# Cached attention for one token: the output weights loaded in two large pieces behind the last K

## The chip, the cores and the metric

The kernel runs on one core of a Trainium2 chip. The metric is the device time of one execution in microseconds (us), the median of several runs. The profile is of one such execution; it names the engines PE (TensorE, matmuls; PEld is its weight load), DVE (VectorE), ACT (ScalarE), POOL (GpSimd) and SP (SyncE, which here only issues transfers).

## The reference

Two independent attention blocks, A and B, each with its own input, caches and weights, are computed and their results put side by side. For each of them, with batch B = 8, one query token, D = 1024, H = 32 heads, Sk = 4096 cached positions and Dh = 128, all bf16:

```python
q = (x @ wq).reshape(B, 1, H, Dh).transpose(0, 2, 1, 3)
p = softmax(einsum("bhqd,bhkd->bhqk", q, k_cache) * Dh ** -0.5)
o = einsum("bhqk,bhkd->bhqd", p, v_cache)
y = o.transpose(0, 2, 1, 3).reshape(B, 1, H * Dh) @ wo
```

The output is `concatenate([yA, yB], axis=-1)`, 8 x 1 x 2048. The caches are 4 x 268 MB, the four weight matrices 8.4 MB each; every byte is read once.

## The kernel before, in words

**Slots.** The work is cut into NS = 64 slots, 32 for A and then 32 for B. A slot is one batch entry with a group of eight heads (HP = 8); four groups (NG) of eight batch entries make a block, and the batch entry runs fastest. A slot's K is 8 heads x 4096 positions x 128, 8 MB (8,388,608 bytes), laid out as 128 partitions x 64 KB: sixteen partitions a head, each with T = 256 positions. Its V has the same form. K goes into one of two buffers (`kbuf`, slot number modulo 2), V into the one buffer `vbuf`. "MB" of a load below means 1,048,576 bytes, "KB" 1024.

**One slot.** VectorE multiplies K by the query, spread over all partitions, in four chunks in place (`multiply`, line 352). TensorE sums the products over Dh with sixteen matmuls a chunk against the identity (`add_up`, line 362) into the banks `red`, and VectorE reduces the rest (line 374). After a softmax whose exponentials are eight ACTIVATEs on ScalarE (`exps`, line 390), the probabilities stand ready for P.V (`pv`, line 413), which a slot later multiplies them with V into the bank `oacc`; `copy_o` (line 432) brings it to SBUF, `gather` (line 442) adds the sixteen partitions of a head, `rowsum` (line 396) sums the exponentials, and `heads` (line 455) divides and files the result, on GpSimd, into `ona` (line 457), a buffer for two groups.

**Order.** The program is written out by hand in one list an engine, and waits are worked out from what each operation reads and writes. In the body of slot n (lines 540 to 601) the loads come first: K of slot n, at times a piece of output weights, V of slot n - 1. SyncE issues them in this order and stops at each until its buffer is free. Then the four chunks pass through VectorE and TensorE, P.V of slot n - 1 follows on TensorE, and the exponentials on ScalarE.

**Output weights before.** Each two heads (256 rows of `wo`, 512 KB) are one load into `wob` (`load_wo`, line 322), two rows of 2 KB that are adjacent in memory for each partition, so 4 KB runs. There are 32 such pairs of heads; 28 of them, all but those of the last group of B, are loaded in this way, one in every second slot from slot 10 on and one in slot 63. In such a slot GpSimd picks the two heads (`pick_heads`, line 461), TensorE permutes them to fit the rows (`permute`, line 468, four matmuls), VectorE copies the result (line 474), TensorE multiplies them with the weights (`project`, line 480, eight matmuls through `strips`, which puts the four quarters of the 1024 columns on four strips of partitions), VectorE copies that (line 491) and GpSimd adds it up in `osum` (lines 494 and 497). When A is complete its four output pieces are stored by SyncE (`store`, in slot 44).

**The last slots before.** In slot 63 the last V is issued directly behind V of slot 62, in four parts (half, quarter, two eighths) into the K buffer of slot 62 (`load_v`, lines 306 to 313). P.V of slot 62 frees `vbuf`, and the last group's weights follow there, four loads of 512 KB in 2 KB runs (`load_wo_last`, line 324). Matmuls on the identity whose result nobody reads (`idle`, line 516) fill TensorE's waits. The last projection (`project_last`) goes part by part as these weights land; VectorE adds `osum` (line 507) and SyncE and ScalarE store the second half.

**Loops.** All slots but the first and the last are hardware loops over two slots: slots 1 to 8, and 9 to 62, which differ by the output weights.

Of the kernel before, what the change touches and what calls it, by code (L numbers as in the profile page):

```python
# [143 lines left out]
def _build(nc, caches, out):  # L144
# [15 lines left out]
    CW = D // 4  # L160
    assert Sq == 1 and Dh == 128 and Sk == 4096 and D == 1024 and H % HP == 0 and B == 8 and NP * 2 == B
    assert R * H * Dh == T * Dh and NC == 2
# [3 lines left out]
    with es:  # L166
# [10 lines left out]
        wob = sb("wob", [128, 2, D], BF16)  # L177
# [8 lines left out]
        ona = sb("ona", [128, 2, HP, B], BF16)  # L186
# [7 lines left out]
        ong = sb("ong", [128, 2, B], BF16)  # L194
        onp = sb("onp", [128, 2, B], BF16)
# [7 lines left out]
        xs = wob[:].rearrange("p a n -> p (a n)").rearrange("p (c n) -> p c n", c=NC)  # L203
        xT = orow[:, 0:NC * R * B].rearrange("p (c r b) -> p c r b", c=NC, r=R)
        qrow = [(asb[:].bitcast(BF16), "asb"), (osum[:].bitcast(BF16), "osum")]
        otail = kbuf[:, 1, 0:2 * TB * Dh].bitcast(FP32)
# [30 lines left out]
        for base, mul in ((0, 1), (SEG - 1, -1)):  # L237
            P.add("pool", lambda e, base=base, mul=mul: e.affine_select(
                out=neg[:], in_=neg[:], compare_op=ALU.is_ge, fill=-1e30, base=base,
                pattern=[[-mul * SEG, HP]], channel_multiplier=mul), reads=["neg"], writes=["neg"])  # L240
        P.add("dve", lambda e: e.memset(ones[:], 1.0), writes=["ones"])
# [11 lines left out]
        def make_xT(c):  # L253
            def emit(e):
                last = None
                for r in range(R):
                    last = e.matmul(sps[:, 256 + r * B:256 + (r + 1) * B], xs[0:B, c, r::R], ident[0:B, 0:B], start=True, stop=True)
                return last
            P.add("pe", emit, reads=[f"xs{c}", "wo", "ident"], banks=["sps"])
            P.add("dve", lambda e: e.tensor_copy(xT[:, c].rearrange("p r b -> p (r b)"), sps[:, 256:256 + R * B]),  # L260
                  writes=["orow"], banks=["sps"])
# [38 lines left out]
        def load_v(m):  # L300
            c, g, b = where(m)
            if m < NS - 1:
                dma("sp", vbuf[:], source(c, 2, b, g), ["v"], "v")
                vplace[m] = (vbuf[:], [("v", 0, T)])
                return
            i, at, parts = NS % 2, 0, []
            for j, w in enumerate((T // 2, T // 4, T // 8, T // 8)):
                name = f"vpart{j}"
                dma("sp", kbuf[:, i, at * Dh:(at + w) * Dh], source(c, 2, b, g)[:, at * Dh:(at + w) * Dh],
                    [name] if j else [name, f"k{i}"], name)  # L310
                parts.append((name, at, w))
                at += w
            vplace[m] = (kbuf[:, i, :], parts)

        def wo_rows(p):
            gi, k = divmod(p, NP)
            c, g = divmod(gi, NG)
            at = (g * HP + 2 * k) * Dh
            return caches[c][4][at:at + 2 * Dh, :]

        def load_wo(p):
            dma("sp", wob[:], wo_rows(p).rearrange("(p j) n -> p j n", j=2), ["wo"], "wo")

        def load_wo_last():
            for k in range(NP):
                name = f"wlast{k}"
                dma("sp", wlast[:, 2 * k:2 * k + 2, :], wo_rows((NC * NG - 1) * NP + k).rearrange("(h p) n -> p h n", p=Dh),
                    [name] if k else [name, "v"], name)
# [99 lines left out]
        def copy_o(m):  # L428
            if m == NS - 2:
                P.add("dve", lambda e: e.tensor_copy(otail, oacc[:]), writes=["k1", "otail"], banks=["oacc"])  # L430
                return
            P.add("act", lambda e: e.activation(osb[:], oacc[:], ACTF.Copy), writes=scores, banks=["oacc"])  # L432

        def gather(m, after=False):
            o = 32 + (m % 2) * HP
            parts = len(vplace[m][1])
            tb, of = (2, olate) if after else (TB, otail if m == NS - 2 else osb)
# [7 lines left out]
            P.add("pe", emit, reads=(["asb"] if after else ["otail"] if m == NS - 2 else scores) + ["sel"], banks=["sps"])  # L445

        def heads(m):
            i = m % 2
            o = 32 + i * HP
            gi, b = divmod(m, B)  # L450
            if m == NS - 1:
                P.add("dve", lambda e: e.tensor_tensor(ona[:, gi % 2, :, b], sps[:, o:o + HP], rl[:, i, :], ALU.mult),
                      reads=[f"rl{i}"], writes=[f"ona{gi % 2}"], banks=["sps"])
# [3 lines left out]
            P.add("pool", lambda e: e.tensor_copy(ona[:, gi % 2, :, b], on[:, i, :]), reads=[f"on{i}"], writes=[f"ona{gi % 2}"])  # L457

        def pick_heads(p):
            gi, k = divmod(p, NP)  # L460
            P.add("pool", lambda e: e.tensor_copy(ong[:], ona[:, gi % 2, 2 * k:2 * k + 2, :]), reads=[f"ona{gi % 2}"], writes=["ong"])

        def permute():
            def emit(e):
                last = None
                for hh in range(2):
                    for j in range(2):
                        last = e.matmul(sps[64 * hh:64 * hh + 64, 64 + j * B:64 + (j + 1) * B], ident[:, j::2], ong[:, hh, :],  # L468
                                        start=True, stop=True, tile_position=(0, 64 * hh))
                return last  # L470
            P.add("pe", emit, reads=["ong", "ident"], banks=["sps"])

        def permuted():
            P.add("dve", lambda e: e.tensor_copy(onp[:].rearrange("p j b -> p (j b)"), sps[:, 64:64 + 2 * B]),
                  writes=["onp"], banks=["sps"])
# [8 lines left out]
        def project():  # L484
            def emit(e):
                strips(e, onp[:, 0, :], wob[:, 0, :], True, False)
                return strips(e, onp[:, 1, :], wob[:, 1, :], False, True)
            P.add("pe", emit, reads=["onp", "wo"], banks=["acc"])

        def projected(p):  # L490
            P.add("dve", lambda e: e.tensor_copy(asb[0:104, :], acc[0:104, 0:CW]), writes=["asb"], banks=["acc"])  # L491
            k = p % (NP * NG)
            if k == 0:
                P.add("pool", lambda e: e.tensor_copy(osum[0:104, :], asb[0:104, :]), reads=["asb"], writes=["osum"])
                return
            dst, name = (orow, "orow") if k == NP * NG - 1 else (osum, "osum")
            P.add("pool", lambda e: e.tensor_tensor(dst[0:104, :], asb[0:104, :], osum[0:104, :], ALU.add),  # L497
                  reads=["asb", "osum"], writes=[name])

        def project_last():  # L500
            g = (NC * NG - 1) % 2
            for k in range(NP):
                def emit(e, k=k):
                    strips(e, ona[:, g, 2 * k, :], wlast[:, 2 * k, :], k == 0, False)
                    return strips(e, ona[:, g, 2 * k + 1, :], wlast[:, 2 * k + 1, :], False, k == NP - 1)
                P.add("pe", emit, reads=[f"ona{g}", f"wlast{k}"], banks=["acc"])
            P.add("dve", lambda e: e.tensor_tensor(orow[0:104, :], acc[0:104, 0:CW], osum[0:104, :], ALU.add),
                  reads=["osum"], writes=["orow"], banks=["acc"])
# [17 lines left out]
        L0, L1, L2 = 1, B + 1, NS - 1  # L526
# [13 lines left out]
        for n in range(NS):  # L540
            m = n - 1
            p = (n - B - 2) // 2 if n >= B + 2 and n % 2 == 0 else NP * (NC * NG - 1) - 1 if n == NS - 1 else None
            if n in (L1, L2):
                for e, at in marks().items():
                    P.loops[e].append((start[e], at, (n - was) // 2))
            if n in (L0, L1):
                start, was = marks(), n
# [30 lines left out]
            add_up(n, 3)  # L578
            reduce(n, 3)
# [20 lines left out]
            if n == B * NG + B + 4:  # L600
                store(0)
# [112 lines left out]
```

## Time and profile before

| What | us |
|---|---|
| median of three runs | 2566.83 (2566.71 to 2567.71) |
| the profiled execution's own time | 2566.92 |
| its span in the profile | 2565.0 |
| busy: PE, DVE, ACT, POOL | 1472.9, 1371.9, 647.2, 314.9 |
| from issue to landing of a 512 KB piece of output weights, median | 51.3 (A), 51.0 (B) |
| from issue to landing of a part of the last group's weights, median | 15.1 |

The span goes from the first to the last instruction; the execution's own time is 1.9 us more. The mean granted TensorE clock was 0.799. In rows of the timeline the columns are start, duration, engine, line, operation, output tile <- input tiles, size and count; a bracket at the end gives the engine's idle time before the row and what ended it. In rows of windows the columns are the stretch and its length, busy time of PE, PEld, DVE, ACT and POOL with the number of instructions, the granted clock, the busy share of the sixteen DMA engines, and GB/s.

### The profile page before, as it was taken

How to read it: one execution, taken by the hardware profiler on the slowest of the kernel's cores; microseconds unless marked ns; L12 is line 12 of the kernel's file. 1: busy time of each engine (PE TensorE's matmuls, PEld its weight loads, DVE VectorE, ACT ScalarE, POOL GpSimd, SP SyncE). 2: the span in 40 equal slices, each digit the busy share in tenths (PEclk: the TensorE clock that was granted, in tenths of full speed). 3: DMA queues.
4: the chain of work that ended last, by engine and by line, in shares of the span. 5: the costliest groups of instructions: out<-in, count | busy, mean ns of one | idle time of the engine just before them, and what ended most of it. 6: DMA issues, size and time to landing. Idle time of an engine off the chain costs nothing.

```text
span 2565.0 us, 19446 instructions
## 1 busy us (share of the span) xinstructions
PE 1472.9 (57%) x9528; PEld 290.1 (11%) x5688; DVE 1371.9 (53%) x969; ACT 647.2 (25%) x1121; POOL 314.9 (12%) x166
## 2 busy tenths in 40 slices
PE   3565565565565555655655556556556565565566
PEld 0101101101111111111110111110101111111102
DVE  3456455465464564554645645546446455465463
ACT  0322322313313223223132132231321322313313
POOL 0101011011011010110110111101101111011010
PEclk8787787787887877878878778778787787787888
DMA  9999999999999999999999999999999999999999
GB/s 425 430 436 432 434 434 432 434 432 433 433 433 431 432 433 433 433 433 433 433 433 433 433 432 434 433 432 432 433 429 439 433 433 432 432 430 432 433 433 392
DMA packets 24445, 1107.54 MB, mean 432 GB/s; under 512 B 2720, under 2 KB 2784, under 8 KB 7408
## 3 DMA queue, kind: packets, MB, share of 16 engines
q1 hardware_dynamic: 24368, 1107.33, 99.9%
q8 instruction: 7, 0.11, 0.0%
q10 hardware_dynamic: 64, 0.04, 0.0%
q14 instruction: 6, 0.05, 0.0%
HBM read 1107.33 MB, written 0.03 MB: 432 GB/s over the span
## 4 chain that ended last, share of the span: by engine, by line
DMA 40%; PE 22%; DVE 18%; another core or an unknown queue 9%; issue 9%; ACT 1%; SPq 0%; DVEq 0%; ACTq 0%
DMA kbuf<-in_A_k_cache_dram 21%; DMA kbuf<-in_B_k_cache_dram 19%; PE red L362 16%; DVE kbuf L352 14%; PE oacc L413 5%; DVE osb L374 2%; ACT prob L390 1%; PE red L516 0%; SPq L223 0%; DVE on L455 0%; DVEq L647 0%; DVE rmax L379 0%; ACT qbc L344 0%; DVE rl L402 0%
## 5 line engine op out<-in xcount | busy, mean ns | idle before, releaser
L352 DVE TENSOR_TENSOR kbuf<-kbuf,qbc 128x8192 bf16<-128x8192 bf16 x256 | 1128.2, 4408 | 807.4 <-DMA kbuf<-in_A_k_cache_dram 363.4
L362 PE MATMUL red<-kbuf,ident 128*128 128x512 bf16 x4096 | 1057.8, 419 | 409.8 <-DVE kbuf L352 206.9
L390 ACT ACTIVATE prob<-osb,bias 128x256 bf16<-128x256 f32 x512 | 598.7, 1583 | 929.3 <-PE oacc L413 894.7
L457 POOL COPY ona<-on 128x8 bf16<-128x8 bf16 x64 | 278.7, 4354 | 1853.6 <-DVE on L455 1853.6
L442 PE MATMUL sps<-sel,osb 128*128 128x8 f32 x504 | 115.6, 358 | 648.4 <-ACT osb L432 648.3
L374 DVE TENSOR_REDUCE osb<-red 128x64 f32<-128x512 f32 x256 | 176.0, 687 | 304.1 <-PE red L362 304.1
L390 ACT ACTIVATION_READ_ACCUMULATOR prob<-osb,bias 128x1 f32 x512 | 252.9, 494 | 0.0
L344 ACT ACTIVATE qbc<-bps 128x256 bf16<-128x256 f32 x32 | 12.3, 384 | 938.9 <-PE bps L340 938.9
L413 PE MATMUL oacc<-vbuf,prob 128*32 128x512 bf16 x4032 | 229.1, 380 | 0.0
L442 PEld LDWEIGHTS sps<-sel,osb 128*128 128x128 f32 x504 | 111.5, 326 | 667.8 <-issue 667.8
L413 PEld LDWEIGHTS oacc<-vbuf,prob 128*32 128x32 bf16 x4032 | 101.8, 97 | 315.2 <-issue 219.0
L362 PEld LDWEIGHTS red<-kbuf,ident 128*128 128x128 bf16 x256 | 25.1, 98 | 974.4 <-issue 948.3
L497 POOL TENSOR_TENSOR osum<-asb,osum 104x256 f32<-104x256 f32 x25 | 18.1, 723 | 309.1 <-DVE asb L491 309.1
L432 ACT ACTIVATE osb<-oacc 128x512 f32<-128x512 f32 x63 | 37.6, 597 | 10.8 <-PE oacc L413 3.8
L396 PE MATMUL sps<-rsum,ones 128*128 128x8 f32 x128 | 36.6, 359 | 5.5 <-ACT prob L390 5.5
L396 PEld LDWEIGHTS sps<-rsum,ones 128*128 128x128 f32 x128 | 34.7, 330 | 6.1 <-ACT prob L390 5.5
L379 DVE TENSOR_REDUCE rmax<-osb 128x1 f32<-128x256 f32 x64 | 26.9, 420 | 7.6
L468 PEld LDWEIGHTS sps<-ong,ident 128*64 128x64 bf16 x112 | 4.1, 109 | 154.9 <-issue 154.9
L380 DVE STREAM_TRANSPOSE tmax<-rmax 128x32 f32<-128x32 f32 x64 | 13.5, 212 | 7.7
L402 DVE RECIPROCAL rl<-sps 128x8 f32<-128x8 f32 x64 | 12.7, 198 | 8.0 <-PE sps L396 8.0
L333 POOL COPY qg<-qT 128x256 bf16<-128x256 bf16 x32 | 12.7, 396 | 28.0 <-DVE qT L286 27.5
L381 DVE TENSOR_REDUCE nmax<-tmax 128x2 f32<-128x32 f32 x64 | 11.9, 186 | 7.6
(59 smaller groups left out, 138.4 us busy)
## 6 DMA issues: line engine op xcount, KB each, us to landing
wob<-in_A_wo_dram SPq DMA_DIRECT2D x16, 512.0 KB, 51.3
wob<-in_B_wo_dram SPq DMA_DIRECT2D x12, 512.0 KB, 51.0
kbuf<-in_B_v_cache_dram SPq DMA_DIRECT2D x1, 4096.0 KB, 42.4
kbuf<-in_B_v_cache_dram SPq DMA_DIRECT2D x1, 2048.0 KB, 47.0
kbuf<-in_B_v_cache_dram SPq DMA_DIRECT2D x2, 1024.0 KB, 49.8
vbuf<-in_B_wo_dram SPq DMA_DIRECT2D x4, 512.0 KB, 15.1
kbuf<-in_A_k_cache_dram SPq DMA_DIRECT2D x32, 50.1
vbuf<-in_A_v_cache_dram SPq DMA_DIRECT2D x32, 31.1
```

What stands on the lines that cost most here:

```text
L352: P.add("dve", lambda e: e.tensor_tensor(kv, kv, qbc[:, n % 2, :].unsqueeze(1).to_broadcast([128, CT, Dh]), ALU.mult), reads=[f"k{n % 2}", ...
L362: first = e.matmul(rv, ident[:], pj[:, :, 0, :], start=True, stop=False).ins
L374: P.add("dve", lambda e: e.tensor_reduce(score[:, ch * CT:(ch + 1) * CT], rv, AX.X, ALU.add), writes=[f"score{ch}"], banks=[f"red{i}"])
L379: P.add("dve", lambda e: e.tensor_reduce(rmax[:], score, AX.X, ALU.max), reads=scores, writes=["rmax"])
L380: P.add("dve", lambda e: e.transpose(tmax[:], rmax[:].to_broadcast([128, 32])), reads=["rmax"], writes=["tmax"])
L390: P.add("act", lambda e, h=h: e.activation(prob[:, :, h], score, ACTF.Exp, bias=bias[:, h:h + 1], scale=scale, accum_out=rsum[:, i, h:h + 1]),
L396: P.add("pe", lambda e: e.matmul(sps[:, i * HP:(i + 1) * HP], ones[:].to_broadcast([128, 128]), rsum[:, i, :], start=True, stop=True), rea ...
L413: last = e.matmul(to[32 * q:32 * q + tb * HP, 0:tb * Dh], prob[:, t:t + tb, :].rearrange("p t h -> p (t h)"), buf[:, t * Dh:(t + tb) * Dh] ...
L432: P.add("act", lambda e: e.activation(osb[:], oacc[:], ACTF.Copy), writes=scores, banks=["oacc"])
L442: last = e.matmul(sps[:, o:o + HP], of[:, t * Dh:(t + 1) * Dh], sel[:, t, :], start=(t == 0 and not after), stop=(t == tb - 1 and (after o ...
L457: P.add("pool", lambda e: e.tensor_copy(ona[:, gi % 2, :, b], on[:, i, :]), reads=[f"on{i}"], writes=[f"ona{gi % 2}"])
L497: P.add("pool", lambda e: e.tensor_tensor(dst[0:104, :], asb[0:104, :], osum[0:104, :], ALU.add), reads=["asb", "osum"], writes=[name])
```

## The change

- **Loads.** The 28 loads of 512 KB are gone. In slot 63, `load_wo(0)` takes all of A's `wo` (8 MB) into the K buffer of slot 62 behind the load of the last K and ahead of V of slot 62: 128 partitions x 32 rows, 64 KB runs. When the projection of A has read it, `load_wo(1)` takes the rows of B's first three groups (6 MB) into the same buffer: 96 partitions x 32 rows, 64 KB runs. The last group's weights are loaded as before.
- **Last V.** It goes, in the same four parts, into the buffer of the last K in place of that of slot 62, and is issued after `load_wo(1)`.
- **Heads.** `ona` keeps the heads of all eight groups. Partition 4h + j of the weights holds rows 32j to 32j + 31 of head h, so the heads are turned (`turn_heads`: eight matmuls against the identity, two copies on ScalarE) and spread (`spread_heads`: four matmuls against `pick`, a matrix that GpSimd makes at the start with two operations, and one copy on ScalarE). This is done in slot 63, for A before and after the second chunk, for B before and after the fourth.
- **Projection.** `project(0)` is 32 x 4 matmuls behind the second chunk of slot 63; ScalarE copies the result and stores all four pieces of A. `project(1)` is 24 heads' worth, 32 x 4 matmuls on 96 partitions, after the exponentials and before the gather of slot 62; its sum stays in the bank `acc`, and the last projection adds to it there, so VectorE's last addition becomes a copy.
- **Loops and the rest.** Slots 1 to 62 are one hardware loop. The input rows `xs` lie in `prob` in place of `wob`. Slot 63's `idle` calls are eight matmuls in place of three and 36; the copy of slot 62's P.V goes to `osb` on ScalarE in place of VectorE.

The core of the diff:

```diff
-        wob = sb("wob", [128, 2, D], BF16)
-        ona = sb("ona", [128, 2, HP, B], BF16)
+        ona = sb("ona", [128, NC * NG, HP, B], BF16)
+        pick = sb("pick", [H, 128 + 3], BF16)
+        turned = sb("turned", [H, B, Dh], BF16)
+        onp = sb("onp", [128, RW, B], BF16)
...
+        wo = kbuf[:, 0, :].rearrange("p (r n) -> p r n", r=RW)
...
-            i, at, parts = NS % 2, 0, []
+            i, at, parts = (NS - 1) % 2, 0, []
...
-        def load_wo(p):
-            dma("sp", wob[:], wo_rows(p).rearrange("(p j) n -> p j n", j=2), ["wo"], "wo")
+        def load_wo(c):
+            k = 128 if c < NC - 1 else 128 - 128 // NG
+            dma("sp", kbuf[0:k, 0, :], caches[c][4][0:k * RW, :].rearrange("(p r) n -> p (r n)", r=RW), ["k0"], "wo")
...
+        def turn_heads(c):
+            k = NG if c < NC - 1 else NG - 1
+            for half, (t, bank) in enumerate(((bps, "bps"), (acc, "acc"))):
+                def emit(e, half=half, t=t):
+                    last = None
+                    for j in range(4):
+                        last = e.matmul(t[0:k * HP, j * Dh:(j + 1) * Dh],
+                                        ona[:, c * NG:c * NG + k, :, 4 * half + j].rearrange("p g h -> p (g h)"), ident[:],
+                                        start=True, stop=True)
+                    return last
+                P.add("pe", emit, reads=[f"ona{c * NG + g}" for g in range(k)] + ["ident"], banks=[bank])
+                P.add("act", lambda e, half=half, t=t: e.activation(
+                    turned[0:k * HP, 4 * half:4 * half + 4, :].rearrange("h b d -> h (b d)"), t[0:k * HP, :], ACTF.Copy),
+                    writes=[f"turned{half}"], banks=[bank])
+
+        def spread_heads(c):
+            k = H if c < NC - 1 else H - HP
+
+            def emit(e):
+                last = None
+                for q in range(QW):
+                    last = e.matmul(bps[0:QW * k, 0:RW * B].rearrange("p (r b) -> p r b", b=B),
+                                    pick[0:k, QW - 1 - q:QW - 1 - q + QW * k],
+                                    turned[0:k, :, q * RW:(q + 1) * RW].rearrange("h b r -> h r b"),
+                                    start=(q == 0), stop=(q == QW - 1))
+                return last
+            P.add("pe", emit, reads=["turned0", "turned1", "pick"], banks=["bps"])
+            P.add("act", lambda e: e.activation(onp[0:QW * k].rearrange("p r b -> p (r b)"), bps[0:QW * k, 0:RW * B], ACTF.Copy),
+                  writes=["onp"], banks=["bps"])
...
+        def project(c):
+            k = 128 if c < NC - 1 else 128 - 128 // NG
+
+            def emit(e):
+                last = None
+                for r in range(RW):
+                    last = strips(e, onp[0:k, r, :], wo[0:k, r, :], r == 0, r == RW - 1 and c < NC - 1)
+                return last
+            P.add("pe", emit, reads=["onp", "k0"], banks=["acc"])
+
+        def projected():
+            P.add("act", lambda e: e.activation(orow[0:104, :], acc[0:104, 0:CW], ACTF.Copy), writes=["orow"], banks=["acc"])
...
-                    strips(e, ona[:, g, 2 * k, :], wlast[:, 2 * k, :], k == 0, False)
+                    strips(e, ona[:, g, 2 * k, :], wlast[:, 2 * k, :], False, False)
...
-            P.add("dve", lambda e: e.tensor_tensor(orow[0:104, :], acc[0:104, 0:CW], osum[0:104, :], ALU.add),
-                  reads=["osum"], writes=["orow"], banks=["acc"])
+            P.add("dve", lambda e: e.tensor_copy(orow[0:104, :], acc[0:104, 0:CW]), writes=["orow"], banks=["acc"])
...
-                dma("sp" if c < NC - 1 or q < 2 else "act", out[:, 0, c * D + q * CW:c * D + (q + 1) * CW],
+                dma("sp" if c == NC - 1 and q < 2 else "act", out[:, 0, c * D + q * CW:c * D + (q + 1) * CW],
...
             if n >= 1:
                 load_k(n)
-            if p is not None:
-                load_wo(p)
-                pick_heads(p)
+            if n == NS - 1:
+                load_wo(0)
             if m >= 0:
                 load_v(m)
...
             add_up(n, 0)
+            if n == NS - 1:
+                turn_heads(0)
             multiply(n, 1)
-            if p is not None:
-                permute()
             reduce(n, 0)
-            if p is not None:
-                permuted()
             add_up(n, 1)
+            if n == NS - 1:
+                spread_heads(0)
+                project(0)
+                projected()
+                store(0)
+                load_wo(1)
             multiply(n, 2)
-            if p is not None:
-                project()
             reduce(n, 1)
             add_up(n, 2)
+            if n == NS - 1:
+                turn_heads(1)
             multiply(n, 3)
             reduce(n, 2)
-            if p is not None:
-                projected(p)
             add_up(n, 3)
+            if n == NS - 1:
+                spread_heads(1)
             reduce(n, 3)
...
                 copy_o(m)
                 if n == NS - 1:
-                    idle(3)
+                    project(1)
+                    idle(8)
                 gather(m)
-            if n == NS - 1:
-                heads(m)
-                idle(36)
             rowsum(n)
```

More of the change, by code (lines that the diff above doesn't have):

```diff
@@ L160, in _build @@
     CW = D // 4
+    RW = H * Dh // 128
+    QW = Dh // RW
     assert Sq == 1 and Dh == 128 and Sk == 4096 and D == 1024 and H % HP == 0 and B == 8 and NP * 2 == B
-    assert R * H * Dh == T * Dh and NC == 2
+    assert R * H * Dh == T * Dh and NC == 2 and QW == 4 and RW * D == T * Dh
     scale = float(Dh) ** -0.5
@@ L193, in _build @@
         on = sb("on", [128, 2, HP], BF16)
-        ong = sb("ong", [128, 2, B], BF16)
-        onp = sb("onp", [128, 2, B], BF16)
         qg = sb("qg", [128, 2, HP, SEG], BF16)
@@ L202, in _build @@
         olate = asb[:, 0:2 * Dh]
-        xs = wob[:].rearrange("p a n -> p (a n)").rearrange("p (c n) -> p c n", c=NC)
+        xs = prob[:].rearrange("p t h -> p (t h)").rearrange("p (c n) -> p c n", c=NC)
+        wo = kbuf[:, 0, :].rearrange("p (r n) -> p r n", r=RW)
         xT = orow[:, 0:NC * R * B].rearrange("p (c r b) -> p c r b", c=NC, r=R)
         qrow = [(asb[:].bitcast(BF16), "asb"), (osum[:].bitcast(BF16), "osum")]
-        otail = kbuf[:, 1, 0:2 * TB * Dh].bitcast(FP32)
         wlast = vbuf[:, 0:HP * D].rearrange("p (h n) -> p h n", h=HP)
@@ L240, in _build @@
                 pattern=[[-mul * SEG, HP]], channel_multiplier=mul), reads=["neg"], writes=["neg"])
+        P.add("pool", lambda e: e.memset(pick[:], 0.0), writes=["pick"])
+        P.add("pool", lambda e: e.affine_select(
+            out=pick[:], in_=pick[:], compare_op=ALU.not_equal, fill=1.0, base=1 - QW,
+            pattern=[[1, 128 + 3]], channel_multiplier=-QW), reads=["pick"], writes=["pick"])
         P.add("dve", lambda e: e.memset(ones[:], 1.0), writes=["ones"])
@@ L258, in emit @@
                 return last
-            P.add("pe", emit, reads=[f"xs{c}", "wo", "ident"], banks=["sps"])
+            P.add("pe", emit, reads=[f"xs{c}", "ident"] + probs, banks=["sps"])
             P.add("dve", lambda e: e.tensor_copy(xT[:, c].rearrange("p r b -> p (r b)"), sps[:, 256:256 + R * B]),
@@ L313, in load_v @@
             vplace[m] = (kbuf[:, i, :], parts)
[L315 to L319, printed above, removed]
-        def load_wo(p):
-            dma("sp", wob[:], wo_rows(p).rearrange("(p j) n -> p j n", j=2), ["wo"], "wo")
+        def load_wo(c):
+            k = 128 if c < NC - 1 else 128 - 128 // NG
+            dma("sp", kbuf[0:k, 0, :], caches[c][4][0:k * RW, :].rearrange("(p r) n -> p (r n)", r=RW), ["k0"], "wo")
         def load_wo_last():
+            rows = caches[NC - 1][4][(NG - 1) * HP * Dh:, :]
             for k in range(NP):
                 name = f"wlast{k}"
-                dma("sp", wlast[:, 2 * k:2 * k + 2, :], wo_rows((NC * NG - 1) * NP + k).rearrange("(h p) n -> p h n", p=Dh),
+                dma("sp", wlast[:, 2 * k:2 * k + 2, :], rows[2 * k * Dh:(2 * k + 2) * Dh, :].rearrange("(h p) n -> p h n", p=Dh),
                     [name] if k else [name, "v"], name)
@@ L428, in copy_o @@
         def copy_o(m):
-            if m == NS - 2:
-                P.add("dve", lambda e: e.tensor_copy(otail, oacc[:]), writes=["k1", "otail"], banks=["oacc"])
-                return
             P.add("act", lambda e: e.activation(osb[:], oacc[:], ACTF.Copy), writes=scores, banks=["oacc"])
@@ L436, in gather @@
             parts = len(vplace[m][1])
-            tb, of = (2, olate) if after else (TB, otail if m == NS - 2 else osb)
+            tb, of = (2, olate) if after else (TB, osb)
             def emit(e):
@@ L444, in emit @@
                 return last
-            P.add("pe", emit, reads=(["asb"] if after else ["otail"] if m == NS - 2 else scores) + ["sel"], banks=["sps"])
+            P.add("pe", emit, reads=(["asb"] if after else scores) + ["sel"], banks=["sps"])
         def heads(m):
@@ L449, in heads @@
             o = 32 + i * HP
-            gi, b = divmod(m, B)
+            gi, b = divmod(m % NS, B)
             if m == NS - 1:
-                P.add("dve", lambda e: e.tensor_tensor(ona[:, gi % 2, :, b], sps[:, o:o + HP], rl[:, i, :], ALU.mult),
-                      reads=[f"rl{i}"], writes=[f"ona{gi % 2}"], banks=["sps"])
+                P.add("dve", lambda e: e.tensor_tensor(ona[:, gi, :, b], sps[:, o:o + HP], rl[:, i, :], ALU.mult),
+                      reads=[f"rl{i}"], writes=[f"ona{gi}"], banks=["sps"])
                 return
@@ L456, in heads @@
                   reads=[f"rl{i}"], writes=[f"on{i}"], banks=["sps"])
[L457 to L463, printed above, removed]
+            P.add("pool", lambda e: e.tensor_copy(ona[:, gi, :, b], on[:, i, :]), reads=[f"on{i}"], writes=[f"ona{gi}"])
@@ L464, in emit @@
+        def spread_heads(c):
+            k = H if c < NC - 1 else H - HP
             def emit(e):
                 last = None
[L466 to L469, printed above, removed]
-                return last
-            P.add("pe", emit, reads=["ong", "ident"], banks=["sps"])
@@ L473, in permuted @@
-        def permuted():
-            P.add("dve", lambda e: e.tensor_copy(onp[:].rearrange("p j b -> p (j b)"), sps[:, 64:64 + 2 * B]),
-                  writes=["onp"], banks=["sps"])
+                for q in range(QW):
[3 more added lines that the diff above has]
+                                    start=(q == 0), stop=(q == QW - 1))
@@ L482, in strips @@
             return last
-        def project():
+        def project(c):
+            k = 128 if c < NC - 1 else 128 - 128 // NG
             def emit(e):
[L486 to L498, printed above, removed]
+                last = None
[5 more added lines that the diff above has]
+            P.add("act", lambda e: e.activation(orow[0:104, :], acc[0:104, 0:CW], ACTF.Copy), writes=["orow"], banks=["acc"])
         def project_last():
-            g = (NC * NG - 1) % 2
+            g = NC * NG - 1
             for k in range(NP):
                 def emit(e, k=k):
-                    strips(e, ona[:, g, 2 * k, :], wlast[:, 2 * k, :], k == 0, False)
+                    strips(e, ona[:, g, 2 * k, :], wlast[:, 2 * k, :], False, False)
                     return strips(e, ona[:, g, 2 * k + 1, :], wlast[:, 2 * k + 1, :], False, k == NP - 1)
                 P.add("pe", emit, reads=[f"ona{g}", f"wlast{k}"], banks=["acc"])
-            P.add("dve", lambda e: e.tensor_tensor(orow[0:104, :], acc[0:104, 0:CW], osum[0:104, :], ALU.add),
-                  reads=["osum"], writes=["orow"], banks=["acc"])
+            P.add("dve", lambda e: e.tensor_copy(orow[0:104, :], acc[0:104, 0:CW]), writes=["orow"], banks=["acc"])
         def idle(k):
@@ L541, in _build @@
             m = n - 1
-            p = (n - B - 2) // 2 if n >= B + 2 and n % 2 == 0 else NP * (NC * NG - 1) - 1 if n == NS - 1 else None
-            if n in (L1, L2):
+            if n == NS - 1:
                 for e, at in marks().items():
-                    P.loops[e].append((start[e], at, (n - was) // 2))
-            if n in (L0, L1):
-                start, was = marks(), n
+                    P.loops[e].append((start[e], at, (n - 1) // 2))
+            if n == 1:
+                start = marks()
             if n >= 1:
                 load_k(n)
-            if p is not None:
-                load_wo(p)
-                pick_heads(p)
+            if n == NS - 1:
+                load_wo(0)
             if m >= 0:
@@ L561, in _build @@
             add_up(n, 0)
+            if n == NS - 1:
+                turn_heads(0)
             multiply(n, 1)
-            if p is not None:
-                permute()
             reduce(n, 0)
-            if p is not None:
-                permuted()
             add_up(n, 1)
+            if n == NS - 1:
[4 more added lines that the diff above has]
+                load_wo(1)
             multiply(n, 2)
-            if p is not None:
-                project()
             reduce(n, 1)
             add_up(n, 2)
+            if n == NS - 1:
+                turn_heads(1)
             multiply(n, 3)
             reduce(n, 2)
-            if p is not None:
-                projected(p)
             add_up(n, 3)
+            if n == NS - 1:
+                spread_heads(1)
             reduce(n, 3)
@@ L593, in _build @@
                 if n == NS - 1:
-                    idle(3)
+                    project(1)
+                    idle(8)
                 gather(m)
-            if n == NS - 1:
-                heads(m)
-                idle(36)
             rowsum(n)
-            if n == B * NG + B + 4:
-                store(0)
+        heads(NS - 2)
         invert(NS - 1)
```

1 line of the change is left out of this document (removed).

## The prediction

> **What bounds the kernel now.** I read the page first: the span, the forty slices with their DMA line, and the queues.
>
> ```profile
> span 2565.0 us, 19446 instructions
> ...
> DMA  9999999999999999999999999999999999999999
> GB/s 425 430 436 432 434 434 432 434 432 433 433 433 431 432 433 433 433 433 433 433 433 433 433 432 434 433 432 432 433 429 439 433 433 432 432 430 432 433 433 392
> DMA packets 24445, 1107.54 MB, mean 432 GB/s; under 512 B 2720, under 2 KB 2784, under 8 KB 7408
> ...
> q1 hardware_dynamic: 24368, 1107.33, 99.9%
> ```
>
> The DMA line is full in every slice, and one queue, SyncE's, fills 99.9% of sixteen engines. No compute engine comes near (PE has 57% of the span). So the time is the price of 1107 MB plus what lies before the first and behind the last byte. What can change it is the price of a byte, a gap in the queue, and the end.
>
> Next come the waits of SyncE's queue, and the page's time from issue to landing of a K load.
>
> ```profile
> SPq L632 <- PE oacc L413: 2379.2, 63, 39.2
> ```
>
> ```profile
> kbuf<-in_A_k_cache_dram SPq DMA_DIRECT2D x32, 50.1
> ```
>
> SyncE stands nearly all the time at the wait for the previous P.V, which frees the V buffer, and then issues the next V and the next K together. A K load lands 50.1 us after its issue, later than the longest wait of 39.2 ends, so K is still under way when the next V joins it: the queue is never empty.
>
> The price of a byte comes from the timeline of VectorE: the first multiply of a slot, where a K load ended its idle time, marks the landing of that K.
>
> ```profile
> 120.78 4.43 DVE L352 TENSOR_TENSOR kbuf<-kbuf,qbc 128x8192 bf16<-128x8192 bf16 x1 [11.91 <-DMA kbuf<-in_A_k_cache_dram]
> ...
> 391.87 4.42 DVE L352 TENSOR_TENSOR kbuf<-kbuf,qbc 128x8192 bf16<-128x8192 bf16 x1 [12.61 <-DMA kbuf<-in_A_k_cache_dram]
> ...
> 470.58 4.42 DVE L352 TENSOR_TENSOR kbuf<-kbuf,qbc 128x8192 bf16<-128x8192 bf16 x1 [13.29 <-DMA kbuf<-in_A_k_cache_dram]
> 509.29 4.43 DVE L352 TENSOR_TENSOR kbuf<-kbuf,qbc 128x8192 bf16<-128x8192 bf16 x1 [11.53 <-DMA kbuf<-in_A_k_cache_dram]
> 549.26 4.42 DVE L352 TENSOR_TENSOR kbuf<-kbuf,qbc 128x8192 bf16<-128x8192 bf16 x1 [13.37 <-DMA kbuf<-in_A_k_cache_dram]
> ...
> 864.00 4.42 DVE L352 TENSOR_TENSOR kbuf<-kbuf,qbc 128x8192 bf16<-128x8192 bf16 x1 [13.72 <-DMA kbuf<-in_A_k_cache_dram]
> ```
>
> ```profile
> 459.51 0.43 SPq L223 DMA_DIRECT2D wob<-in_A_wo_dram  x1
> ```
>
> From 470.58 to 509.29 one V and one K landed: 38.71 us for two loads of 8 MB in 64 KB runs, so **19.36 us for a full load**, and 2.42 for each of the eight partitions that one DMA engine carries. The load of output weights issued at 459.51 stands behind a K in the queue, so it falls in the next stretch, 509.29 to 549.26: 39.97 us. **Its 512 KB in 4 KB runs cost 1.26 us**; at the price of the long runs they would be 38.71 / 32 = 1.21.
>
> The end, from the SyncE, VectorE and TensorE timelines:
>
> ```profile
> 2466.16 0.43 SPq L223 DMA_DIRECT2D kbuf<-in_B_k_cache_dram  x1
> 2490.39 0.33 SPq L223 DMA_DIRECT2D wob<-in_B_wo_dram  x1
> 2503.86 0.33 SPq L223 DMA_DIRECT2D vbuf<-in_B_v_cache_dram  x1
> 2504.24 1.86 SPq L223 DMA_DIRECT2D kbuf<-in_B_v_cache_dram  x4
> 2544.11 4.30 SPq L223 DMA_DIRECT2D vbuf<-in_B_wo_dram  x4
> 2562.73 0.68 SPq L223 DMA_DIRECT2D out_dram<-orow  x2
> ```
>
> ```profile
> 2516.30 4.43 DVE L352 TENSOR_TENSOR kbuf<-kbuf,qbc 128x8192 bf16<-128x8192 bf16 x1 [13.81 <-DMA kbuf<-in_B_k_cache_dram]
> ...
> 2562.28 0.42 DVE L507 TENSOR_TENSOR orow<-acc,osum 104x256 bf16<-104x256 f32 x1 [1.22 <-PE acc L480]
> ```
>
> ```profile
> 2561.10 1.12 PE L480 MATMUL acc<-vbuf,ona 128*8 128x256 bf16 x32
> 2561.83 0.11 PEld L480 LDWEIGHTS acc<-vbuf,ona 128*8 128x8 bf16 x8 [0.19 <-DMA vbuf<-in_B_wo_dram]
> ```
>
> The last K lands at 2516.30. Behind it in the queue are one weight load, the V of slot 62, the V of slot 63 and the last group's weights, whose last part releases PE at 2561.83; 3.2 us later the span ends. So the end too waits for a transfer, not for an engine.
>
> **The change part by part.**
>
> *Removed from the loop.* 28 loads of 512 KB and, beside each, twelve small matmuls, two copies on VectorE, two operations on GpSimd. The engine work I cost at nothing: VectorE sits idle 11 to 14 us before each K (the brackets above), and what hides it, the DMA stream, stays. The loads are 28 x 1.26 = 35.3 us.
>
> *Added behind the last K.* One load of 8 MB and one of 6 MB, both in 64 KB runs. The bytes are the same. At the long-run price they are 19.36 + 14.52 = 33.9. **Gain 1.4 us.** Bounds: taken from longer stretches, a pair of slots with a load lasts (864.00 - 470.58) / 5 = 78.68 and without one 2 x (391.87 - 120.78) / 7 = 77.45, so a load is 1.23 and the gain 28 x 0.023 = 0.6. The other end is the nearest row of shorter runs, the last group's weights in 2 KB runs:
>
> ```profile
> 2558.00:2560.00 2.00, 1.90 (x25) 1.37 (x25) 0.00 (x0) 0.29 (x1) 0.00 (x0) 1.00 1.01 370
> ```
>
> At 370 GB/s 512 KB take 1.42, or 0.21 more than 1.21; with half as many runs 0.10 more, and 28 of these are 2.9 us. I keep 1.4, from the row of the load itself, and 0.6 to 2.9 for the range.
>
> *The 6 MB load has 96 partitions.* Every large load in this trace has 128, so no row has its price. The lower bound is three quarters of a full load, 14.52. [...] I take **19.36, that is 4.84 us more**, the middle one, which equals a row of the trace.
>
> [...]
>
> *The new order at the end.* 27 loads no longer stand before the last K, so it lands at 2516.3 - 27 x 1.26 = 2482. K of slot 62, whose buffer the 8 MB take, is summed before that, so the queue goes on with the 8 MB (landing 2501.6), V of slot 62 (2521.0), the 6 MB (2535.5 to 2540.4), V of slot 63 (19.36 more) and the last group's weights, which are unchanged. Three waits are new on SyncE:
>
> - The 6 MB wait for the first projection, and V of slot 63 and the last weights stand behind that wait. The projection is 32 rows x 4 matmuls; 32 matmuls took 1.12 us above, so 128 take 4.5, or 9.0 at half clock. From 2501.6 it ends at 2506 to 2511. V of slot 62 keeps the queue busy until 2521.0: at least 10 us of cover.
> - V of slot 63 now goes into the last K's own buffer, so it waits until that is summed: two more rounds of sixteen matmuls behind the projection, 3.6 to 5.9 us each (below), so 2513 to 2523. Cover until 2535.5.
> - The last weights wait for P.V of slot 62, at 2521.0 plus 3.6: 2525, again under the 6 MB.
>
> ```profile
> 2520.79 5.91 PE L362 MATMUL red<-kbuf,ident 128*128 128x512 bf16 x16 [4.41 <-DVE kbuf L352]
> ...
> 2536.82 3.63 PE L362 MATMUL red<-kbuf,ident 128*128 128x512 bf16 x16 [1.30 <-DVE kbuf L352]
> 2540.38 3.64 PE L413 MATMUL oacc<-vbuf,prob 128*32 128x512 bf16 x64
> ```
>
> The turning and spreading of the heads (24 matmuls and six copies on ScalarE) are done before the weights land. The second projection, 96 matmuls in 3.4 to 6.7 us from 2535.5 or 2540.4, has the 19.36 us of V of slot 63 above it. The eight matmuls on the last part, the copy in place of the addition (0.42), and the stores stay: 3.2 us. Where a cover of 10 us or more were gone, each us over it would be a us of the end.
>
> *The stores of the first half* go to ScalarE, which idles then, and the two new operations on GpSimd at the start end long before the first K. Nothing.
>
> **The sum**, against the profiled execution's 2566.92: -1.4 + 4.84 = +3.4, so **2570.4 us**. The median of the runs shown, 2566.83, is 0.1 away, so I take it as it is.
>
> **The rivals.**
>
> *The 6 MB go at three quarters.* Rows are dealt six to an engine and none disturbs another. For it: 96 divides by sixteen. [...] Time: 2566.9 - 1.4 = 2565.5, with the bounds of the gain 2564.0 to 2566.3.
>
> [...]
>
> *A gap in the queue.* SyncE is in order; if the first projection ended after 2521, all that is behind would slide. It needs 10 us more than half clock gives. For it: PE has idled before it. Time at 5 us of gap: 2575 or later.
>
> *The change does not do what it says*, that is, 4 KB runs cost nothing over 64 KB: gain 0.6 or none, within the first two cases.
>
> **How the numbers follow.** Forecast (19.36 for the 6 MB, 2568.9 to 2571.2) 0.33; three quarters 0.30; engines in each other's way 0.25; a gap, or rows dealt worse still, 0.08; something else 0.04. The first two lie within 0.2% of 2566.8 (5.1 us, about what a measurement of this kernel can tell from no change), but for a little of the first. So same 0.60, slower 0.37, faster 0.03, since the most that the runs can give is 2.9 us. The range takes the first three cases: 2564.0 to 2581.0. The likeliest alone: 2568.9 to 2571.2.
>
> **What would show it.** The pitch of K landings in the loop should be 38.7 throughout, without the 39.97. The last K should land near 2482. [...] A hole with no queue busy is the gap. PE's last eight matmuls should still be released by the last weights. I am wrong if the last K lands far from 2482, or if PE, not a DMA, ends the wait before the last matmuls.

## The result, and the profile after

The changed kernel takes **2581.82 us** (median of six runs, 2581.35 to 2582.06), the kernel before 2566.86 in the same series: the ratio is 1.0058, 95% interval 1.0045 to 1.0071. It is slower by 15.0 us. The forecast was 2570.4, the range ended at 2581.0.

The first lines of the page of the changed kernel:

```profile
span 2580.3 us, 19022 instructions
...
DMA  9999999999999999999999999999999999999999
GB/s 422 436 427 436 437 428 436 437 428 436 436 430 435 436 430 435 435 431 435 435 431 435 435 431 435 435 431 435 435 432 434 435 432 434 435 432 434 435 432 275
DMA packets 20668, 1107.53 MB, mean 429 GB/s; under 512 B 2304, under 2 KB 2368, under 8 KB 3408
```

The DMA line is as full as before in every slice, the last one too. The GB/s line is not: the last slice falls to 275, where it was 392. So the engines are busy to the end, but move less. The loss is all in the last 64 us.

The loop went as worked out. VectorE's timeline has the landings of the last two K loads:

```profile
2443.24 4.42 DVE L354 TENSOR_TENSOR kbuf<-kbuf,qbc 128x8192 bf16<-128x8192 bf16 x1 [11.79 <-DMA kbuf<-in_B_k_cache_dram]
2481.87 4.43 DVE L354 TENSOR_TENSOR kbuf<-kbuf,qbc 128x8192 bf16<-128x8192 bf16 x1 [12.29 <-DMA kbuf<-in_B_k_cache_dram]
```

The pitch is 38.63, and the last K lands 34.4 us earlier than before (2516.30). Behind it, the SyncE timeline shows when each load could be issued, and TensorE's shows, by what ended its idle time, when each landed:

```profile
2467.36 0.33 SPq L225 DMA_DIRECT2D kbuf<-in_A_wo_dram  x1
2470.94 0.33 SPq L225 DMA_DIRECT2D vbuf<-in_B_v_cache_dram  x1
2507.60 0.34 SPq L225 DMA_DIRECT2D kbuf<-in_B_wo_dram  x1
2515.33 1.76 SPq L225 DMA_DIRECT2D kbuf<-in_B_v_cache_dram  x4
2528.80 12.60 SPq L225 DMA_DIRECT2D vbuf<-in_B_wo_dram  x4
```

```profile
2501.34 6.21 PE L491 MATMUL acc<-kbuf,onp 128*8 128x256 bf16 x128 [3.81 <-DMA kbuf<-in_A_wo_dram]
...
2523.13 5.56 PE L415 MATMUL oacc<-vbuf,prob 128*32 128x512 bf16 x64 [6.05 <-DMA vbuf<-in_B_v_cache_dram]
...
2552.01 6.47 PE L491 MATMUL acc<-kbuf,onp 96*8 96x256 bf16 x128 [23.32 <-DMA kbuf<-in_B_wo_dram]
```

The 8 MB of A landed 19.5 us after the last K, a full load's price. The 6 MB were issued at 2507.60, with V of slot 62 still 15 us from landing, and the last V at 2515.33: no wait left a hole. But V of slot 62 took 21.8 us, and the 6 MB **28.9** behind it: 50.7 us for the two, where 33.9 is the price of their bytes. Windows inside that stretch (the last two columns are the DMA share and GB/s):

```profile
2506.00:2516.00 10.00, 10.00 (x86) 1.96 (x49) 1.38 (x2) 1.45 (x3) 0.00 (x0) 0.97 1.04 448
2526.00:2531.00 5.00, 2.69 (x40) 0.97 (x32) 0.00 (x0) 2.19 (x5) 0.00 (x0) 0.89 0.97 210
2541.00:2546.00 5.00, 0.00 (x0) 0.00 (x0) 0.00 (x0) 0.00 (x0) 0.00 (x0) 0.50 1.00 210
2551.00:2556.00 5.00, 3.99 (x76) 2.71 (x80) 0.00 (x0) 0.00 (x0) 0.00 (x0) 0.50 0.91 390
```

While the 6 MB pass, the queue moves 210 GB/s in place of 433, and its share still reads 1.00. All sixteen engines are at work, at half pace.

The account of the 15.3 us between the two spans: from the landing of the last K to the end, 98.4 us stand where 48.7 stood (2580.3 - 2481.87, 2565.0 - 2516.30), 49.7 more, and that K lands 34.4 earlier. In the 98.4, the two loads above have 16.8 more than the price of their bytes. The rest of the 49.7 is the 14 MB of output weights that now stand there (33.9), less the one load of 512 KB that stood there before (1.3), and 0.3 more.

### The profile page after: what moved, and what is told of

Same layout as the page of the kernel before. It is cut to its first block, busy times and chain, and to the rows that moved or that the text cites. A ratio compares the mean times of both kernels' runs of the same rounds, so it can differ in the third digit from the quotient of the medians.

```text
span 2580.3 us, 19022 instructions
## 1 busy us (share of the span) xinstructions
PE 1469.4 (57%) x9441; PEld 292.7 (11%) x5601; DVE 1359.5 (53%) x912; ACT 651.1 (25%) x1129; POOL 291.2 (11%) x112
## 4 chain that ended last, share of the span: by engine, by line
DMA 62%; PE 17%; DVE 14%; issue 5%; another core or an unknown queue 0%; SPq 0%; ACT 0%; DVEq 0%; ACTq 0%
DMA kbuf<-in_B_k_cache_dram 30%; DMA kbuf<-in_A_k_cache_dram 28%; PE red L364 12%; DVE kbuf L354 12%; PE oacc L415 4%; DMA kbuf<-in_B_v_cache_dram 2%; DVE osb L376 2%; DMA kbuf<-in_A_wo_dram 1%; SPq L225 0%; ACT prob L392 0%; PE acc L491 0%; DVE on L454 0%; DVEq L652 0%; PE sps L441 0%
## 5 line engine op out<-in xcount | busy, mean ns | idle before, releaser
L454 DVE TENSOR_TENSOR on<-sps,rl 128x8 bf16<-128x8 f32 x64 | 10.1, 158 | 44.3 <-PE sps L398 44.3
L491 PE MATMUL acc<-kbuf,onp 128*8 128x256 bf16 (+1 forms) x256 | 12.7, 390 | 27.1 <-DMA kbuf<-in_B_wo_dram 23.3
L385 DVE SCALAR_TENSOR_TENSOR bias<-nmax,neg 128x8 f32<-128x8 f32 x64 | 10.7, 167 | 7.7
```

What stands on the lines that cost most here:

```text
L491: last = e.matmul(acc[32 * q:32 * q + B, 0:CW], vec, w[:, q * CW:(q + 1) * CW], start=begin, stop=end, tile_position=(0, 32 * q))
```

## The experiments

**Theory (rows):** the loss is the pace of the load itself, which on 96 partitions is half that of a load on 128 (210 GB/s against 433). **Rival (order):** the loss is a stall behind the new waits, or comes of the last V's new place or of A's stores beside the load. Kernels given without a range below (e3, e4, e5, e7 and e8) were run once. The runs of each of the others spread by 2 us at most, so only differences well above that are read from single times, and smaller ones from the traces.

### The second load on all 128 partitions (e1_full_rows)

```diff
-            k = 128 if c < NC - 1 else 128 - 128 // NG
+            k = 128
```

> The changed kernel, but the second load of output weights takes all 128 partitions, 8 MB in place of 6 MB, in the same 64 KB runs, to the same buffer, behind the same waits; the projection still uses the first 96. [...] In the changed kernel V of slot 62 and the 6 MB landed 50.7 us after the 8 MB of A (2501.3 to 2552.0); two full loads should take 38.7, though 2 MB more are moved. So about 2581.8 - 12 = 2570. Rival (order): the loss is a stall of the queue behind the new waits, or the stores of A on the second queue beside it: the load then goes at the same pace of 210 GB/s, 40 us for 8 MB, and the time rises to about 2592.

Measured: 2570.34 us (ten runs, 2570.04 to 2571.09), ratio to the kernel before 1.0013 (1.0003 to 1.0023). TensorE's timeline:

```profile
2501.25 5.33 PE L491 MATMUL acc<-kbuf,onp 128*8 128x256 bf16 x128 [2.81 <-DMA kbuf<-in_A_wo_dram]
...
2520.85 5.98 PE L415 MATMUL oacc<-vbuf,prob 128*32 128x512 bf16 x64 [4.74 <-DMA vbuf<-in_B_v_cache_dram]
2540.30 6.49 PE L491 MATMUL acc<-kbuf,onp 96*8 96x256 bf16 x128 [13.47 <-DMA kbuf<-in_B_wo_dram]
```

With a third more bytes the load takes 19.4 us in place of 28.9, and V ahead of it 19.6 in place of 21.8. Every wait is where it was. The rival fell here: 2 MB more made the kernel 11.5 us faster. And 2570.34 is the sum of the forecast (2570.4), which had this load at 19.36: its other terms hold together.

### The second load left out (e3_no_6mb)

```diff
-                load_wo(1)
```

> The changed kernel without the load of 6 MB; the projection of B's first three groups then uses what lies in the buffer, so the output of B is not the reference's. All other waits and work stay. It gives the marginal price of the load. Theory (rows): V of slot 62 lands 19.4 after A's weights, as any full load, and the last V follows at once: 50.7 - 19.4 = 31.3 us less, 2550.5. Rival (order, the load itself at the common pace of 14.5): 2567. If V of slot 62 itself still takes 21.8 us, what slows it is not this load.

Measured: 2552.47, so the load is worth 29.4 us. V of slot 62 now lands at its ordinary price:

```profile
2501.25 6.54 PE L491 MATMUL acc<-kbuf,onp 128*8 128x256 bf16 x128 [3.57 <-DMA kbuf<-in_A_wo_dram]
...
2520.58 5.32 PE L415 MATMUL oacc<-vbuf,prob 128*32 128x512 bf16 x64 [3.25 <-DMA vbuf<-in_B_v_cache_dram]
...
2536.16 1.88 PE L441 MATMUL sps<-sel,osb 128*128 128x8 f32 x8 [4.93 <-ACT osb L431]
...
2538.40 4.63 PE L415 MATMUL oacc<-kbuf,prob 128*32 128x512 bf16 x56
```

That is 19.3 after A's weights, so the 2.3 us more that V cost in the changed kernel belong to the load behind it. The time is 2 us over the 2550.5 expected. The last two rows show why: with the load gone, the first three parts of the last V are multiplied in one go (x56), with no idle time put down to a transfer. The wait ahead of them, 4.93 us, was ended by ScalarE. The end has become a chain of ScalarE and TensorE.

### K of slot 0 in pieces: the cost by itself

Three kernels take the kernel before and change one load, 2500 us away from the output weights; VectorE's multiplies wait for all its pieces.

```diff
+            if n == 0:
+                dma("sp", kbuf[0:64, 0, :], source(c, 1, b, g)[0:64], ["k0h"], "k0h")
+                dma("sp", kbuf[64:128, 0, :], source(c, 1, b, g)[64:128], ["k0"], "k0")
+                return
```

> The kernel before, but K of slot 0 is loaded in two transfers, partitions 0 to 63 and 64 to 127, directly one behind the other on the same queue; nothing else differs. The disputed cost by itself, far from the output weights. Theory (rows): each half of 4 MB goes at half pace and takes 19.4, so 19.4 us more in all: 2566.9 + 19.4 = 2586.3, and windows of the first 50 us show about 210 GB/s while the DMA share stays full. Rival (order or source): 64 partitions go as 128 do, 2566.9.

Measured: 2589.52, 22.7 us more than before and 3.3 more than the 19.4 worked out. At 210 GB/s 8 MB take 39.9 us, which is 20.6 more than 19.36, and the load ahead (`wq`) landed 1.0 later (23.77 against 22.74); 1.1 us stay open. Two of its windows:

```profile
30.00:40.00 10.00, 1.51 (x38) 1.00 (x34) 1.71 (x3) 1.67 (x2) 0.80 (x2) 0.64 1.02 210
50.00:60.00 10.00, 0.00 (x0) 0.00 (x0) 0.00 (x0) 0.00 (x0) 0.00 (x0) 0.50 1.02 210
```

The second kernel has the cut at 96 in place of 64.

> The kernel before, but K of slot 0 is loaded in two transfers, partitions 0 to 95 and 96 to 127. [...]

Measured: 2589.42, the same as with halves. Its windows from 25 to 60 us lie at 210 to 213 GB/s; two of them:

```profile
30.00:40.00 10.00, 1.35 (x34) 0.99 (x34) 1.32 (x3) 1.67 (x2) 0.80 (x2) 0.61 1.00 210
50.00:60.00 10.00, 0.00 (x0) 0.00 (x0) 0.00 (x0) 0.00 (x0) 0.00 (x0) 0.50 1.03 210
```

So this 96-partition load went at half pace from end to end.

The third asks whether it is the number of partitions.

```diff
+            if n == 0:
+                for at, to, name in ((32, 96, "k0a"), (0, 32, "k0b"), (96, 128, "k0")):
+                    dma("sp", kbuf[at:to, 0, :], source(c, 1, b, g)[at:to], [name], name)
+                return
```

> The kernel before, but K of slot 0 is loaded in three transfers: partitions 32 to 95, 0 to 31, 96 to 127. What decides, the number of partitions or which ones? [...]

Measured: 2579.05, 12.0 us more than before. Windows of the first transfer and of the two small ones:

```profile
20.00:30.00 10.00, 6.22 (x64) 1.95 (x64) 0.36 (x1) 0.00 (x0) 0.00 (x0) 1.00 0.97 419
35.00:40.00 5.00, 0.00 (x0) 0.00 (x0) 0.00 (x0) 0.08 (x1) 0.00 (x0) 0.50 1.02 210
45.00:50.00 5.00, 0.00 (x0) 0.00 (x0) 0.00 (x0) 0.00 (x0) 0.00 (x0) 0.50 1.02 210
```

Partitions 32 to 95 went at full pace, 419 GB/s; 0 to 63 did not, with 210. So it is not the number of partitions alone. The two sets differ in where they lie: 0 to 63 lie all below 64, 32 to 95 half below and half above. The two pieces of 32 partitions went at half pace, 210.

### The 96 rows shifted (e8_96_shifted)

```diff
-            dma("sp", kbuf[0:k, 0, :], caches[c][4][0:k * RW, :].rearrange("(p r) n -> p (r n)", r=RW), ["k0"], "wo")
+            a = 16 * c
+            dma("sp", kbuf[a:a + k, 0, :], caches[c][4][0:k * RW, :].rearrange("(p r) n -> p (r n)", r=RW), ["k0"], "wo")
```

> The changed kernel, but the 96 rows of B's weights go to partitions 16 to 111 in place of 0 to 95; the projection still reads 0 to 95, so the output of B is not the reference's. Below and above partition 64 there are then 48 rows each. [...] If only the share of the lower and the upper 64 partitions counts, it is 14.5 us and 2566.

Measured: 2581.93, as without the shift, and 210 GB/s in the windows of the load:

```profile
2531.00:2536.00 5.00, 0.00 (x0) 0.00 (x0) 0.00 (x0) 5.00 (x9) 0.00 (x0) 0.61 0.99 210
2541.00:2546.00 5.00, 0.00 (x0) 0.00 (x0) 0.00 (x0) 0.00 (x0) 0.00 (x0) 0.50 1.00 210
```

Half above and half below 64 does not rescue 96 partitions, so the share on each side does not decide alone. What else does is not shown.

One rival stays untested. In e4, e5 and e7 a piece with other partitions also has other rows of the source. Only e8 moves the partitions and not the source, and there the time did not change. So no run here tells whether the place in SBUF or the place in the source makes the difference between 0 to 63 and 32 to 95.

### The 6 MB on 128 partitions in shorter runs (e2b_16kb)

The rows are dealt over all partitions, three runs of 16 KB in each, and the heads are spread to fit. The matrix that spreads them lies in `osum`, which is free by then; with a buffer of its own (e2_16kb) the kernel did not fit into SBUF, and there is no time for it.

```diff
+            if c == NC - 1:
+                dma("sp", kbuf[:, 0, 0:3 * 8 * D].rearrange("p (g m) -> p g m", g=3),
+                    caches[c][4][0:3 * 8 * 128, :].rearrange("(g p r) n -> p g (r n)", g=3, r=8), ["k0"], "wo")
+                return
...
+                    for g in range(3):
+                        for q in range(16):
+                            last = e.matmul(bps[:, g * 64:(g + 1) * 64].rearrange("p (r b) -> p r b", b=B),
+                                            pick16[0:k, 128 * g + 15 - q:128 * g + 143 - q],
+                                            turned[0:k, :, q * 8:(q + 1) * 8].rearrange("h b r -> h r b"),
+                                            start=(q == 0), stop=(q == 15))
```

> The changed kernel, but the 6 MB of B are dealt over all 128 partitions, three runs of 16 KB (eight rows) in each; the heads are spread to fit with 48 small matmuls in place of 4, and the projection is 24 rows x 4 matmuls on 128 partitions. Theory (rows): the load takes 14.5 us, so V of slot 62 and it take 33.9 in place of 50.7, and the time is 2581.8 - 16.8 = 2565.0, that is the kernel before less the gain of the long runs (0.6 to 2.9), unless the end, where TensorE's clock is half, gives up to 1 us back: 2564 to 2566.5. Rival (order): the waits and the late issue of the last V remain and cost what they did, 2575 or more.

Measured: 2565.76 against 2567.04, ratio 0.9996 (0.9987 to 1.0005). TensorE's timeline:

```profile
2520.77 6.52 PE L419 MATMUL oacc<-vbuf,prob 128*32 128x512 bf16 x64 [0.33 <-DMA vbuf<-in_B_v_cache_dram]
2535.51 5.12 PE L509 MATMUL acc<-kbuf,onp 128*8 128x256 bf16 x96 [8.21 <-DMA kbuf<-in_B_wo_dram]
...
2552.50 1.04 PE L419 MATMUL oacc<-kbuf,prob 128*32 128x512 bf16 x8 [1.04 <-DMA kbuf<-in_B_v_cache_dram]
...
2559.29 1.88 PE L509 MATMUL acc<-vbuf,ona 128*8 128x256 bf16 x32
```

The load lands 14.7 us behind V, three quarters of a full load. Everything else of the change is in this kernel, the waits and the last V's place too; the whole 15 us are gone. That leaves a difference to the kernel before of -1.3 in the medians, where the gain had been put at 1.4; the interval does not exclude zero. The spans are clearer: 2563.5 to 2564.0 in the eleven runs, 2564.9 to 2566.8 in those of the kernel before, 1.4 us apart in the medians.

### The end kept warm (e6_16kb_warm)

```diff
+                if m == NS - 1 and k < wide - 1:
+                    idle((18, 8)[k])
...
+        idle(14)
```

> The kernel e2b_16kb with TensorE kept busy while it waits for the parts of the last V: 14, 18 and 8 more matmuls on the identity, whose result nobody reads, ahead of the first, second and third part. In the changed kernel the last 32 matmuls ran at half clock (1.88 us where 1.12 stood before) and so did the gathers ahead of them. Theory (end): where the chain of small matmuls behind the last V part sets the end, this gives about 1 us against e2b_16kb, 2564.0; where the last weights' landing sets it, only the last eight matmuls gain, 0.2 to 0.4 us. Rival: the extra matmuls hold up a part of V and nothing is won.

Measured: 2565.41 (all eleven runs between 2565.20 and 2565.72), ratio to the kernel before 0.9993 (0.9984 to 1.0002).

```profile
2553.07 1.90 PE L543 MATMUL red<-ident 128*128 128x512 bf16 x8
2554.90 0.62 PE L419 MATMUL oacc<-kbuf,prob 128*32 128x512 bf16 x8
...
2559.39 1.07 PE L511 MATMUL acc<-vbuf,ona 128*8 128x256 bf16 x32
```

The last projection takes 1.07 in place of 1.88 us, but starts 0.1 later, since the filling held up the third part of V: it began at 2552.50 in e2b_16kb and at 2554.90 here. The medians differ by 0.35. That this lies in the range of the smaller of the two answers is luck: in neither kernel is a wait before the last matmuls put down to the last weights. It is the quickest kernel here that does all the work, by 1.6 us against before in the medians, 0.06%.

## Why the prediction was wrong, point by point

- **What bounds the kernel** held: the DMA stream, in every slice, before and after.
- **The gain of the long runs** held. 27 loads fewer brought the last K 34.4 us forward, 1.28 each where 1.26 was taken, and the last K landed at 2481.87 where 2482 was forecast. e2b_16kb has the gain without the loss: 1.3 us in the medians, which is not clear of the noise, and 1.4 in the spans.
- **The new waits** held as covers. The 6 MB were issued at 2507.60 (2506 to 2511 forecast), the last V at 2515.33 (2513 to 2523), the last weights at 2528.80, a little late (2525), since V of slot 62 was and its P.V took 5.56 in place of 3.6. No hole opened; the rival of a gap is out.
- **The 6 MB load is the step that failed.** The lower bound was 14.52, and 19.36 was taken, "which equals a row of the trace". No run shows 19.36 for 96 partitions: the load measured 28.9 us, and 29.0 at partitions 16 to 111. It also cost 2.3 us more in the V ahead of it, 16.8 in all where 4.84 was taken. The share stood at 1.00 and the queue at 210 GB/s, so all sixteen engines were busy at half pace. The case "engines in each other's way" had 0.25; it names a cause that no view shows. The range stopped at 2581.0, 0.8 below the result, with no margin for what such a load does to its neighbour. Choosing a price because it looked like a known row was no evidence for it: the row that it equalled was of 128 partitions.
- **Which partitions** explains part. In 64 KB runs, 0 to 63 and 64 to 127 had 210 GB/s and 32 to 95 had 419. The 96 partitions had 210 at both places, and took 28.9 and 29.0 us (2551.72 - 2522.74 in e8_96_shifted, the rows below). No view names the engine that carries a row, so why some sets of partitions went at half pace is not shown. Eight partitions of 128 to an engine, or six of 96, are even shares by sixteen: an estimate.

```profile
2522.74 6.56 PE L416 MATMUL oacc<-vbuf,prob 128*32 128x512 bf16 x64 [6.71 <-DMA vbuf<-in_B_v_cache_dram]
...
2551.72 5.74 PE L492 MATMUL acc<-kbuf,onp 96*8 96x256 bf16 x128 [22.41 <-DMA kbuf<-in_B_wo_dram]
```

- **What would show it**: the DMA share did not show the loss. It stayed at 1.00 and the GB/s halved. It was forecast that the last weights release the last eight matmuls. In the changed kernel all 32 run in one go behind VectorE's last heads, which themselves waited for TensorE (VectorE's timeline, then TensorE's):

```profile
2575.38 0.19 DVE L451 TENSOR_TENSOR ona<-sps,rl 128x8 bf16<-128x8 f32 x1 [13.74 <-PE sps L441]
...
2575.66 1.88 PE L491 MATMUL acc<-vbuf,ona 128*8 128x256 bf16 x32
```

So the second sign of being wrong came true: engines, not a transfer, end the wait. The chain of small matmuls behind the last V, at a granted clock of 0.50, ends a little later than the last weights, which landed at 2576.6 (issued at 2541.0, 35.6 to landing). It cost little: from that landing to VectorE's copy are 1.0 us, where 0.5 stood before (2561.83 to 2562.28).
- **Chances**: "same" had 0.60 and "slower" 0.37; the result is slower by 0.58%.

## What to carry to other kernels

A load that leaves partitions out need not be cheaper by the bytes that it leaves out: here 6 MB on 96 partitions took 28.9 us and 8 MB on 128 took 19.4. Of the narrower loads tried, only partitions 32 to 95 kept the full pace (419 GB/s, the others 210). Where a load has to be smaller, shorter runs on all 128 partitions are worth trying: here 16 KB runs cost next to nothing (14.7 us for 6 MB, where its share of a full load is 14.5). And where no row of a trace has the price of a step, the range should reach past the outer bound, not stop at it.

## What the runs showed of the hardware that was not expected

- A full DMA share said nothing of the pace here: 1.00 at 433 GB/s (the kernel before, 15 to 20 us) and 1.00 at 210 (the changed one, 2541 to 2546).
- The load at half pace slowed the load ahead of it: V of slot 62 took 21.8 us, and 19.3 when the 6 MB behind it were gone.
- In 64 KB runs, 64 partitions went at 210 GB/s as 0 to 63 and as 64 to 127, and at 419 as 32 to 95; 32 partitions went at 210, as 0 to 31 and as 96 to 127; 96 at 210 in both places tried.
- SyncE took 4.30 us to issue the four loads of the last weights before, 12.60 in the changed kernel and 25.38 in e1_full_rows. What sets this no run isolates. It cost nothing here, since nothing waited behind them on SyncE before the last stores.
